# Loading a weight matrix in whole rows and copying it on chip, and holding one load of x back

## The chip, the core and the metric

The kernel runs on one core of a Trainium2 chip. The core has five engines that run their own instruction streams: TensorE (PE, matrix products; PEld is its weight load), VectorE (DVE), ScalarE (ACT), GpSimd (POOL) and SyncE (SP). Here SP and POOL also issue the transfers, which a set of 16 DMA engines carries out. SBUF is the on-chip memory with 128 partitions, PSUM the accumulators that TensorE writes.

The metric is the device time of one execution in microseconds, the median over several runs. The kernel before takes 698.39 us (three runs, 698.24 to 699.26).

## The reference

A short causal convolution, whose seven taps are a softmax over the kernel positions of each of 8 heads, feeds a two-layer network with a leaky ReLU between. Sizes: x is 8 x 4096 x 192 in float32, w_in is 192 x 2048, w_out is 2048 x 192.

```python
w = softmax(weight)                                   # 8 heads x 7 taps
x_pad = concatenate([zeros(B, 6, D), x])              # along the sequence
out = einsum('hk,bskhg->bshg', w, x_unf)              # head h owns 24 of the 192 channels
h = out.reshape(B * S, D) @ w_in
g = maximum(0.01 * h, h)
result = (g @ w_out).astype(float32)
```

## The kernel before

**Tiles.** Channels lie on partitions. The 192 channels make three chunks of 64 (`NCH = 3`, `CH = 64`), and two rows of the batch are processed together: row e=0 on partitions 0 to 63, row e=1 on partitions 64 to 127. A block is 512 positions of such a pair; there are 32. The first five blocks (`NHALF`) are worked in halves of 256 positions. Below, "half 0" to "half 3" are the first four: they are the first entries of `groups`, and the number is also the argument q of `load_first`. The outer loop runs over the groups with index i.

**Why w_in is needed twice in SBUF.** In `mm1` (L361) each row is a product of 64 partitions by 128 columns. For row e, both operands are read from partitions e\*64 to e\*64+63: `w_in[ps, c, ...]` and `y[ps, c, ...]`. So w_in stands in SBUF as [128, 3, 2048] in bf16, the same contents in both halves of the partitions. The copy in memory is float32; POOL's DMA converts it on the way.

**How w_in is loaded.** L234 to L241: four quarters of 512 columns, and for each one load for e=0 and one for e=1, all three chunks in one load. That makes eight DMAs on POOL's queue, each 64 partitions x 3 pieces of 2 KB. w_out follows on the same queue (L243).

**The start.** SP's queue takes the small `weight`, then x of halves 0 and 1 (`load_first`, L107, two DMAs each). A stage pool of two buffers holds these x tiles (`x_nat`). x of half 2 is issued at L335, after an explicit dependence on ScalarE's instruction `low` (L326). x of half 3 is issued at L340 and, as the pool has two buffers, waits until half 1's buffer has been read. `cast_first` turns each into bf16, `transpose_first` turns it on TensorE, and `evac_first` copies it into `xt`.

**The steady order.** For group i, the inner loop has T/64 steps. In each step TensorE runs `mm1` for two values of u, and ScalarE follows with one Prelu per u (L378), which turns the PSUM tile `ph` into `g`. Two `ph` buffers exist. Then come the slots of `mm2` (L391, product with w_out, operating on groups before), and VectorE gets a share of the convolution (L176, L182) of group i+1. In a half, one u covers 256 of the 2048 columns, so all 8 values of u need all of w_in. For half 0 the second matrix product has nothing to do yet; it starts in the first step of i=1. Inside i=0, after u=3, TensorE also does one chunk of the convolution of half 1 (`pe_ahead`). After the last step of i=0 come the cast of half 2's x on VectorE, its transposes and its copies to `xt`. In i=1 ScalarE casts half 3's x after u=0 and after u=2 (L462).

SP's queue is in program order: after the loads of the start it takes the output transfers and the transposing transfers of later blocks. POOL's queue goes on with `load_x` for block 2 and later (L79). It first waits, through a one-element copy (`pjunk`, L475), for the last g of half 0.

Of the kernel before, what the change touches and what calls it, by code (L numbers as in the profile page):

```python
# [14 lines left out]
def kernel(  # L15
# [8 lines left out]
    nc = tc.nc  # L24

    B, S, D = x.shape
    H, K = weight.shape
    Din, F = moe_w_in.shape
# [6 lines left out]
    CH = 64  # L35
    NCH = D // CH
# [5 lines left out]
    NB = S // ST  # L42
    NBLK = (B // 2) * NB
    LAG = NFC + NFC // 2
    WQ = 4
    NHALF = 5
    NPEC = 2

# [58 lines left out]
    def load_first(q, after=None):  # L107
        t = stage_pool.tile([128, 2, HS, D], FP32, name="x_nat")
        for e in range(2):
            ins = nc.sync.dma_start(  # L110
                out=t[:, e, :, :],
                in_=x[e, q * HT : (q + 1) * HT, :].rearrange("(c p) d -> p c d", p=128),
            )
            if after is not None and e == 0:
                tc.add_manual_dep(
                    ins.ins, after.ins.name,
                    mybir.DependencyInfo(
                        mybir.DependencyClass.Sync, mybir.DependencyReason.DATA
                    ),
                    reason="leave the DMA engines to w_in",  # L120
                )
        x_nat[q] = t

    def cast_first(q, e, copy):
        if q % 2 == 0 and e == 0:
            x_bf[q // 2] = xb_pool.tile([128, NCH, SUB, 2, CH], BF16, name="x_bf")
        h = q % 2
        copy(  # L128
            out=x_bf[q // 2][:, :, h * HS : (h + 1) * HS, e, :],
            in_=x_nat[q][:, e, :, :].rearrange("p s (c k) -> p c s k", c=NCH),  # L130
        )
# [20 lines left out]
    def evac_first(q, *copies):  # L152
        dst = xt[0][:, :, HALO + q * HT : HALO + (q + 1) * HT].rearrange(
            "p c (s i k) -> p i s c k", s=HS, i=2
        )
        for i, t in enumerate(ptr.pop(q)):
            copies[i](out=dst[:, i], in_=t)  # L157
# [4 lines left out]
    def conv_jobs(grp, chunks=range(NCH)):  # L162
        blk, t0, T = grp
        rp, st = divmod(blk, NB)
        if blk not in yt:
            yt[blk] = yt_pool.tile([128, NCH, ST], BF16, name="yt")
        y = yt[blk]
        jobs = []
        for c in chunks:
            for k in range(K):  # L170
                a = BASE + k + st * ST + t0
                src = xt[rp][:, c, a : a + T]
                dst = y[:, c, t0 : t0 + T]
                if k == 0:
                    jobs.append(
                        lambda s=src, d=dst, c=c: nc.vector.tensor_scalar_mul(  # L176
                            d, s, wk[:, c, 0:1]
                        )
                    )
                else:  # L180
                    jobs.append(
                        lambda s=src, d=dst, c=c, k=k: nc.vector.scalar_tensor_tensor(  # L182
                            out=d, in0=s, scalar=wk[:, c, k : k + 1], in1=d,
                            op0=mybir.AluOpType.mult, op1=mybir.AluOpType.add,
                        )
                    )
        return jobs
# [39 lines left out]
    for sign, off in ((1, 0), (-1, GRP - 1)):  # L227
        nc.gpsimd.affine_select(  # L228
            out=sel, in_=sel, compare_op=mybir.AluOpType.is_ge, fill=0.0,
            base=off, channel_multiplier=-sign * GRP,  # L230
            pattern=[[sign * CH, NCH], [0, 2], [sign, CH]],
        )

    w_in = const_pool.tile([128, NCH, F], BF16)  # L234
    for q in range(WQ):
        for e in range(2):
            fs = slice(q * F // WQ, (q + 1) * F // WQ)
            nc.gpsimd.dma_start(  # L238
                out=w_in[e * CH : (e + 1) * CH, :, fs],
                in_=moe_w_in[:, fs].rearrange("(c p) f -> p c f", p=CH),  # L240
            )  # L241
    w_out = const_pool.tile([128, NFC, D], BF16)
    nc.gpsimd.dma_start(out=w_out, in_=moe_w_out.rearrange("(c p) d -> p c d", p=128))  # L243

# [3 lines left out]
    def warm(n):  # L248
# [9 lines left out]
        out=nmax, in_=w9[:, 0:K], axis=mybir.AxisListType.X,  # L258
# [3 lines left out]
        out=w9[:, 0:K], in_=w9[:, 0:K], func=mybir.ActivationFunctionType.Exp,  # L262
# [33 lines left out]
    def diag_high(c):  # L296
        nc.vector.tensor_mul(
            diag[c][:, 0],
            ident2[:, None, :].to_broadcast([128, K, CH]),
            whm[:, c, 0, 0:K, None].to_broadcast([128, K, CH]),  # L300
        )

    def diag_low(c, ks):
        for k in ks:
            act = nc.scalar.activation(  # L305
                out=diag[c][:, 1, k, :], in_=ident2,
                func=mybir.ActivationFunctionType.Copy, scale=whm[:, c, 1, k : k + 1],
            )
        return act

    diag_high(0)
    cast_first(0, 0, nc.vector.tensor_copy)
    diag_low(0, range(2))
    cast_first(0, 1, nc.scalar.copy)
    transpose_first(0)
# [7 lines left out]
    wk = const_pool.tile([128, NCH, K], FP32, name="wk")  # L323
    nc.vector.tensor_mul(wk, wraw[:, :, 0:K], rsum.to_broadcast([128, NCH, K]))
    evac_first(0, nc.vector.tensor_copy, nc.scalar.copy)
    low = diag_low(0, range(2, K))  # L326
    diag_high(1)
    diag_low(1, range(K))

    def act_scale(out, in_, scale):  # L330
# [1 line left out]
            out=out, in_=in_, func=mybir.ActivationFunctionType.Copy, scale=scale  # L332
        )

    load_first(2, low)  # L335
    for n, job in enumerate(conv_jobs(groups[0], range(NPEC, NCH))):
        if n in (4, 5):
            cast_first(1, n - 4, nc.vector.tensor_copy)
        job()
    load_first(3)  # L340
    for c in range(NPEC):
        pe_jobs, evac_y = pe_conv_jobs(groups[0], c)
        for job in pe_jobs:
# [17 lines left out]
    def mm1(grp, u):  # L361
        blk, t0, T = grp
        y = yt[blk]
        nf = ST // T
        ph = psum_h.tile([128, 2, ST], FP32, name="ph", tag="ph")
        for i in range(nf):
            f = nf * u + i
            for c in range(NCH):
                for e in range(2):
                    ps = slice(e * CH, (e + 1) * CH)  # L370
                    nc.tensor.matmul(  # L371
                        out=ph[:, e, i * T : (i + 1) * T],
                        lhsT=w_in[ps, c, f * 128 : (f + 1) * 128],
                        rhs=y[ps, c, t0 : t0 + T],
                        start=(c == 0),
                        stop=(c == NCH - 1),
                    )
        act = nc.scalar.activation(  # L378
            out=g[blk][:, nf * u : nf * (u + 1), :, t0 : t0 + T],
            in_=ph.rearrange("p e (i t) -> p i e t", i=nf),  # L380
            func=mybir.ActivationFunctionType.Prelu, alpha=0.01,
        )
        while unsealed:
            seal[unsealed.pop()] = act.ins.name

    def mm2_one(rt, m, fc):
        b, e, s = subs[m]
# [52 lines left out]
    for i, grp in enumerate(groups):  # L440
        blk, t0, T = grp
        steps = T // 64
        if t0 == 0:
            g[blk] = g_pool.tile([128, NFC, 2, ST], BF16, name="g", tag="g")
        quota = (avail - slot) // steps

        if i == 0:
            ahead = []
        else:
            ahead = conv_jobs(groups[i + 1]) if i + 1 < len(groups) else []  # L450
        per = -(-len(ahead) // (steps - 1)) if T == ST else -(-len(ahead) // steps)
        for j in range(steps):
            for u in range(2 * j, 2 * j + 2):
                mm1(grp, u)
                if i == 0 and u == 0:
                    pe_ahead, evac_y = pe_conv_jobs(groups[1], 0)
                    ahead = conv_jobs(groups[1], range(1, NCH))
                    per = len(ahead)
                if i == 0 and u == 3:
                    for job in pe_ahead:  # L460
                        job()
                if i == 1 and u in (0, 2):  # L462
                    cast_first(3, u // 2, nc.scalar.copy)
            for _ in range(quota):
                mm2_slot(slot)
                slot += 1
            if i == 0 and j == 3:
                evac_y(nc.vector.tensor_scalar_mul)
                for e in range(2):
                    cast_first(2, e, nc.vector.tensor_copy)  # L470
                transpose_first(2)
                evac_first(2, nc.vector.tensor_copy, nc.vector.tensor_copy)
            if i == 1 and j == 1:

                nc.gpsimd.tensor_copy(out=pjunk, in_=g[0][0:1, NFC - 1, 1, HT - 1 : HT])  # L475
                load_x(2)
            if i == 2 and j == 1:
                transpose_x(2)
            for job in ahead[per * j : per * (j + 1)]:
                job()  # L480
            if i == 1 and j == 1:
                transpose_first(3)
                evac_first(3, nc.vector.tensor_copy, nc.vector.tensor_copy)

            last_half = t0 + T == ST
            if j == steps // 4 and last_half:
                load_x(blk + 3)
            if j == steps // 2 and last_half and blk > 0:
                transpose_x(blk + 2)
        avail += 2 * T // 128 * NFC  # L490
# [37 lines left out]
```

## Time and profile before

| What | Value |
|---|---|
| Median of the runs | 698.39 us |
| The profiled execution, its own time | 699.96 us |
| The profiled execution, first to last instruction (span) | 698.3 us |
| Mean granted TensorE clock | 0.997 |
| w_in loads, issue on POOL, eight | 626 ns each at the median, from 2.9 us to 8.0 us |
| w_in loads, issue to landing | 6.6 / 8.7 / 11.6 us (least, median, most) |
| w_out load, issue to landing | 14.7 us, from 9.77 us |
| x loads of the start (`x_nat`), issue to landing | 2.5 / 5.6 / 9.3 us |
| TensorE's wait for w_out | 1.8 us, once |
| TensorE's waits for w_in | 2.2 us at the weight load, 0.4 us at the matmul |
| HBM read | 29.88 MB |

The page gives each engine's busy time, then 40 equal slices of the span with tenths of busy time. In those slices the first tenth of the span has the highest DMA share (9, 9, 6, 9, 5), and TensorE is at 9 in all slices but the first and the last. Matmul spans overlap, so 9 means only that it always had work. The chain of work that ended last is followed back from the last instruction. "Issue to landing" is from the start of the issuing instruction to the moment when the last part of that transfer was reported as complete. The answers by stage give sums of busy time inside a stretch, in microseconds from the start of the span. The granted clock there is a share of TensorE's full clock.

### The profile page before, as it was taken

Reading aid. Unit: us, or ns where it says so; the run is one execution under the profiler, and the core shown is the slowest. Engines: PE = TensorE matmul, PEld = TensorE weight load, DVE = VectorE, ACT = ScalarE, POOL = GpSimd, SP = SyncE. Lnnn points to the kernel's source line nnn. Section 1 sums busy time; section 2 is a strip of 40 time slices with the busy share of each in tenths; the row PEclk is TensorE's granted clock in tenths of the full one; section 3 lists DMA queues with packets and bytes.
Section 4 is the critical chain, followed back from the end, with each engine's and each line's share of the span. In section 5 each row is a group of like instructions: output and inputs, shape, how many; then the busy total and the mean of one; then the engine's idle time right before and its main releaser. Section 6 shows DMA issues by size and latency. Waiting matters only on the chain.

```text
span 698.3 us, 26019 instructions
## 1 busy us (share of the span) xinstructions
PE 689.0 (99%) x11762; PEld 608.0 (87%) x11762; DVE 542.1 (78%) x1005; ACT 512.1 (73%) x576; POOL 142.3 (20%) x199
## 2 busy tenths in 40 slices
PE   8899999999999999999999999999999999999997
PEld 6799999678888888888888888888888888888887
DVE  7799999967777787777787777787777787777712
ACT  6688888977777777777777777777777777777770
POOL 4722220410222210222211222220222211000000
PEclk9999999999999999999999999999999999999999
DMA  9969554845555535555645556544566625122112
GB/s 170 115 83 104 83 71 81 86 71 76 77 74 83 89 67 76 77 74 84 86 67 79 69 81 81 88 73 71 77 75 81 92 63 77 54 52 58 47 36 69
DMA packets 184847, 54.39 MB, mean 78 GB/s; under 512 B 148384, under 2 KB 184736, under 8 KB 184736
## 3 DMA queue, kind: packets, MB, share of 16 engines
q0 software_dynamic: 98768, 14.17, 29.5%
q1 hardware_dynamic: 85968, 38.56, 23.2%
q8 instruction: 92, 1.51, 0.9%
q14 instruction: 19, 0.16, 0.1%
HBM read 29.88 MB, written 25.17 MB: 79 GB/s over the span
## 4 chain that ended last, share of the span: by engine, by line
PE 94%; DMA 3%; DVE 2%; POOL 0%; issue 0%; ACT 0%; POOLq 0%; ACTq 0%
PE po L391 48%; PE ph L371 46%; DMA w_out<-in_moe_w_out_dram 2%; DVE yt L182 2%; DMA w_in<-in_moe_w_in_dram 1%; POOL sel L228 0%; DVE yt L176 0%; ACT g L378 0%; POOL sel L226 0%; DVE o_sb L430 0%; POOL ident masks.py:199 0%; POOL ident masks.py:197 0%; PE ptr L143 0%; POOLq masks.py:199 0%; ACTq L430 0%
## 5 line engine op out<-in xcount | busy, mean ns | idle before, releaser
L378 ACT ACTIVATE g<-ph 128x1024 bf16<-128x1024 f32 x512 | 496.4, 1021 | 165.7 <-PE ph L371 165.7
L182 DVE SCALAR_TENSOR_TENSOR yt<-xt,wk,yt 128x512 bf16<-128x512 bf16 (+1 forms) x648 | 442.4, 683 | 17.6
L391 PE MATMUL po<-w_out,g 64*128 64x192 bf16 (+1 forms) x8048 | 398.4, 243 | 1.8 <-DMA w_out<-in_moe_w_out_dram 1.8
L391 PEld LDWEIGHTS <-g 64*128 64x128 bf16 (+1 forms) x8048 | 372.3, 94 | 31.1 <-issue 2.2
L371 PE MATMUL ph<-yt,w_in 64*128 64x512 bf16 (+1 forms) x3552 | 393.6, 348 | 2.2 <-ACT g L378 1.2
L371 PEld LDWEIGHTS <-w_in 64*128 64x128 bf16 x3552 | 247.8, 94 | 50.4 <-issue 3.9
L79 POOL DMA_DIRECT2D x_bf<-in_x_dram x180 | 133.7, 774 | 422.4 <-DMA xt<-x_bf 422.4
L430 DVE COPY o_sb<-po 128x192 f32<-128x192 f32 x216 | 77.2, 357 | 127.4 <-PE po L391 125.0
L176 DVE TENSOR_SCALAR yt<-xt,wk 128x512 bf16<-128x512 bf16 (+1 forms) x108 | 36.3, 336 | 0.1
L430 ACT COPY o_sb<-po 128x192 f32<-128x192 f32 x40 | 13.1, 327 | 0.0
L250 PE MATMUL warm<-zero 128*128 128x256 bf16 x24 | 5.2, 371 | 1.1 <-DVE junk L218 1.1
L157 DVE COPY xt<-ptr 128x384 bf16<-128x384 bf16 x7 | 2.2, 351 | 4.4 <-PE ptr L143 4.4
L201 PE MATMUL acc<-xt,diag 64*64 64x256 bf16 x84 | 5.2, 270 | 0.1
L238 POOL DMA_DIRECT2D w_in<-in_moe_w_in_dram x8 | 5.1, 643 | 0.0
L201 PEld LDWEIGHTS <-diag 64*64 64x64 bf16 x84 | 4.3, 106 | 0.8 <-DVE xt L157 0.4
L305 ACT ACTIVATE diag<-ident,whm 128x64 bf16<-128x64 bf16 x14 | 3.6, 335 | 1.9 <-DVE whm L291 1.9
L250 PEld LDWEIGHTS <-zero 128*128 128x128 bf16 x24 | 2.6, 125 | 2.1 <-DVE junk L218 1.1
L475 POOL COPY pjunk<-g 1x1 bf16<-1x1 bf16 x1 | 0.3, 312 | 10.9 <-ACT g L378 10.9
L143 PEld LDWEIGHTS <-x_bf 64*128 64x128 bf16 x48 | 1.4, 94 | 1.0 <-ACT x_bf L128 0.8
L143 PE MATMUL ptr<-ident,x_bf 64*128 64x64 bf16 x48 | 1.7, 191 | 0.5 <-DVE wraw L318 0.5
L128 DVE CAST x_bf<-x_nat 128x384 bf16<-128x384 f32 x5 | 2.2, 449 | 0.0
L255 ACT ACT_TABLE_LOAD x1 | 1.3, 1283 | 0.8 <-PEq L512 0.8
(34 smaller groups left out, 12.2 us busy)
## 6 DMA issues: line engine op xcount, KB each, us to landing
out_dram<-o_sb SPq DMA_DIRECT2D x128, 192.0 KB, 2.2
x_bf<-in_x_dram POOLq DMA_DIRECT2D x180, 64.0 KB, 3.1
x_nat<-in_x_dram SPq DMA_DIRECT2D x8, 192.0 KB, 5.6
w_in<-in_moe_w_in_dram POOLq DMA_DIRECT2D x8, 192.0 KB, 8.7
xt<-x_bf SPq DMA_TRANSPOSE x90, 2.4
w_out<-in_moe_w_out_dram POOLq DMA_DIRECT2D x1, 768.0 KB, 14.7
w<-in_weight_dram SPq DMA_DIRECT2D x1, 0.2 KB
```

Source lines behind the costliest of these rows:

```text
L79: nc.gpsimd.dma_start(out=t[:, c, :, e, :], in_=src[2 * rp + e, :, :, c * CH : (c + 1) * CH],)
L143: nc.tensor.transpose(out=ts[i][:, s, c, :], in_=x_bf[q // 2][ps, c, (q % 2) * HS + s, :, :].rearrange("p e k -> p (e k)"), identity=ident ...
L176: lambda s=src, d=dst, c=c: nc.vector.tensor_scalar_mul(d, s, wk[:, c, 0:1])
L182: lambda s=src, d=dst, c=c, k=k: nc.vector.scalar_tensor_tensor(out=d, in0=s, scalar=wk[:, c, k : k + 1], in1=d, op0=mybir.AluOpType.mult, ...
L201: lambda k=k, p=p, a=a, e=e, ps=ps: nc.tensor.matmul(out=acc[ps, :T], lhsT=diag[c][ps, p, k, :], rhs=xt[0][ps, c, a : a + T], start=(k == ...
L238: nc.gpsimd.dma_start(out=w_in[e * CH : (e + 1) * CH, :, fs], in_=moe_w_in[:, fs].rearrange("(c p) f -> p c f", p=CH),)
L250: nc.tensor.matmul(out=wa[:, 0, 0:HT], lhsT=zero[:, 0:128], rhs=zero, start=True, stop=True)
L305: act = nc.scalar.activation(out=diag[c][:, 1, k, :], in_=ident2, func=mybir.ActivationFunctionType.Copy, scale=whm[:, c, 1, k : k + 1],)
L371: nc.tensor.matmul(out=ph[:, e, i * T : (i + 1) * T], lhsT=w_in[ps, c, f * 128 : (f + 1) * 128], rhs=y[ps, c, t0 : t0 + T], start=(c == 0) ...
L378: act = nc.scalar.activation(out=g[blk][:, nf * u : nf * (u + 1), :, t0 : t0 + T], in_=ph.rearrange("p e (i t) -> p i e t", i=nf), func=my ...
L391: ins = nc.tensor.matmul(out=po[m], lhsT=g[b][ps, fc, e, s * 128 : (s + 1) * 128], rhs=w_out[ps, fc, :], start=(rt != 1 and fc == 0), stop ...
L430: copy(out=o_sb[:, n % 2, :], in_=po.pop(n))
```

## The change

Three things are changed.

w_in is fetched in three DMAs on POOL's queue, one for each chunk of 64 channels. Each writes partitions 0 to 63 with whole rows of 2048 columns. Three further DMAs on SP's queue copy each chunk from partitions 0 to 63 to partitions 64 to 127. They read what the first three wrote, so SP waits for the landing of each before it issues the copy.

x of half 2 no longer depends on `low`. It stands in SP's queue behind the three copies.

x of half 3 is issued later in the program: inside the main loop at i=0, u=2. It depends on the Prelu of that u, which `mm1` now returns.

```diff
-    WQ = 4
@@ load_first
-                    reason="leave the DMA engines to w_in",
+                    reason="leave the DMA engines to the weights",
@@
     w_in = const_pool.tile([128, NCH, F], BF16)
-    for q in range(WQ):
-        for e in range(2):
-            fs = slice(q * F // WQ, (q + 1) * F // WQ)
-            nc.gpsimd.dma_start(
-                out=w_in[e * CH : (e + 1) * CH, :, fs],
-                in_=moe_w_in[:, fs].rearrange("(c p) f -> p c f", p=CH),
-            )
+    for c in range(NCH):
+        nc.gpsimd.dma_start(out=w_in[0:CH, c, :], in_=moe_w_in[c * CH : (c + 1) * CH, :])
+    for c in range(NCH):
+        nc.sync.dma_start(out=w_in[CH:128, c, :], in_=w_in[0:CH, c, :])
     w_out = const_pool.tile([128, NFC, D], BF16)
     nc.gpsimd.dma_start(out=w_out, in_=moe_w_out.rearrange("(c p) d -> p c d", p=128))
@@ diag_low
-            act = nc.scalar.activation(
+            nc.scalar.activation(
...
-        return act
@@
-    low = diag_low(0, range(2, K))
+    diag_low(0, range(2, K))
@@
-    load_first(2, low)
+    load_first(2)
...
-    load_first(3)
@@ mm1
+        return act
@@ main loop
-                mm1(grp, u)
+                act = mm1(grp, u)
...
+                if i == 0 and u == 2:
+                    load_first(3, act)
```

## The prediction

> **What bounds the kernel now.** The page first: its busy table and its chain that ended last.
>
> ```profile
> span 698.3 us, 26019 instructions
> PE 689.0 (99%) x11762; PEld 608.0 (87%) x11762; DVE 542.1 (78%) x1005; ACT 512.1 (73%) x576; POOL 142.3 (20%) x199
> PE 94%; DMA 3%; DVE 2%; POOL 0%; issue 0%; ACT 0%; POOLq 0%; ACTq 0%
> ```
>
> TensorE sets the time; the only foreign link of any size is 3% DMA. The chain of the first 40 us places it:
>
> ```profile
> 2.90 6.58 DMA w_in<-in_moe_w_in_dram
> 9.48 0.28 issue
> 9.77 14.70 DMA w_out<-in_moe_w_out_dram
> 24.47 0.04 issue
> 24.51 1.33 PE po L391 x14
> ```
>
> POOL issued all eight w_in loads by 8.0, but w_out only at 9.77, after the first w_in load landed (9.48). w_out needed 14.7 us more, and TensorE, done with ph of the second half's first step at 22.4 us, stood until 24.47. Then the table by stage (PE, PEld, DVE, ACT, POOL busy, clock, DMA share, GB/s):
>
> ```profile
> 22.30:25.60 3.30, 1.50 (x23) 1.30 (x19) 3.12 (x7) 1.88 (x3) 3.30 (x5) 1.00 0.93 67
> 25.70:29.00 3.30, 3.30 (x32) 2.45 (x28) 1.46 (x3) 1.51 (x3) 3.30 (x6) 0.50 1.38 87
> 29.10:35.50 6.40, 6.40 (x146) 6.40 (x146) 4.76 (x11) 4.60 (x6) 6.39 (x9) 1.00 1.43 92
> 35.50:46.00 10.50, 10.50 (x230) 9.79 (x226) 9.82 (x24) 8.58 (x13) 0.00 (x0) 1.00 0.50 79
> ```
>
> The stand costs twice: after a stretch with 1.5 of 3.3 us busy the clock is at 0.50 for 3.4 us. From 29 us TensorE is full. So the change can only shift the point from which it is full, and everything behind it moves along. Last, VectorE's timeline for the third half (i=2), which becomes ready at the very end of this stretch:
>
> ```profile
> 20.70 0.62 DVE L157 COPY xt<-ptr 128x384 bf16<-128x384 bf16 x2 [1.14 <-PE ptr L143]
> 30.49 0.62 DVE L157 COPY xt<-ptr 128x384 bf16<-128x384 bf16 x2 [3.23 <-PE ptr L143]
> 32.61 3.09 DVE L182 SCALAR_TENSOR_TENSOR yt<-xt,wk,yt 128x256 bf16<-128x256 bf16 x6
> ```
>
> Its last convolution ends at 35.70; TensorE begins that half at 35.53 and waits 0.2 us for yt in the list of waits. VectorE also stood 3.2 us before 30.49, behind TensorE's stand. I use **35.7 us, third half ready** as the mark to compare.
>
> [...]
>
> **The change, part by part.**
>
> *POOL.* Eight issues of 0.64 us become three. Taken at the old 0.63 us each they end at 2.90+1.9=4.8, and w_out, ninth before and held by the first landing, is fourth: it is issued near 4.8 instead of 9.77.
>
> *Bytes.* w_in was fetched twice in float32, 8 x 0.39 = 3.15 MB; now 1.57 MB, plus 3 x 0.26 MB of bf16 copied on chip.
>
> *When the low half of w_in is in.* The DMA view, in stretches that hold one issue each, gives issue to landing of 6.6, 6.8, 7.1 and 8.4 us for the first four w_in loads, issued at 2.90, 3.65, 4.27 and 4.89: landings at 9.5, 10.4, 11.4 and 13.3. Four loads are 1.57 MB, just what the new kernel fetches. The fourth ran beside half 2's x, whose packets start at 11.5; at the spacing of the first three (0.95) it is 12.3. That is the upper value. The lower comes from two one-microsecond views:
>
> ```profile
> q0 software_dynamic: 103, 0.10, 84.1%
> q0 software_dynamic: 205, 0.19, 121.1%
> ```
>
> These are 6 to 7 us and 9 to 10 us. While the first two loads ran, both 2 KB slices of the same columns, half the bytes moved (0.10 against 0.19 MB of bf16). If whole rows remove this, 4 us at half rate become 2.3, so 10.6. I take 11.3 for the last chunk, some 10.1 and 9.0 for the others. Against it: half 1's x shares the queue with larger pieces; it landed at 8.3, and up to 1.5 us more is hidden, as yt then ends at 12.7 instead of 11.2, before any weights are whole.
>
> *The copies.* SP waits for each chunk in order, then issues. A 192 KB x load took 2.5 us alone, its first packet 1.0 us after issue. Half 2's came 3.5 us after issue, behind w_in packets of 1.211 x 16 / 205 = 95 ns. The copies stand behind w_out packets:
>
> ```profile
> q0 software_dynamic: 498, 0.19, 158.6%
> ```
>
> This is 20 to 21 us: 51 ns each, so about half of those 2.5 us, 1.3. [...]so 2.5+1.3 = 3.8, with 0.1 for SP's wait. Bounds: 2.5 (nothing ahead) to 5.5 (the three queue, 2 x 1.3 less the spacing of the chunks). w_in is whole at T = 11.3+3.9 = **15.2 us**. Until then TensorE has only two matmuls per piece, from about 11.3.
>
> *From T to the mark.* In the kernel before, ph's first matmul that had everything ran at 11.27, the first ACTIVATE of g at 12.03, and the third half's x was in place (evac at 20.70, ends 21.32) 9.3 us after that. In these 9.3 ScalarE waited 0.24 and 0.64 us for ph that w_in held up; these go. So T+0.7+8.4 = T+9.1. TensorE idles some 4 us before T, more than the 3.3 us that cost it half the clock before, so I add that: at half clock 12 matmuls of one u take 1.3 us, not 0.66, against ScalarE's 0.97 per u; 2.6 u in 3.4 us lose 0.9. Then VectorE: three chunks of seven convolution instructions, 3.33 each (21.35 to 24.68 in its timeline), are 10.0, and the copies of half 3 0.6. The mark is T+9.1+0.9+10.6 = T+20.6 = 35.8. TensorE itself arrives a little earlier: it is done with ph of the second half's first step at T+0.7+9.5+0.9 = T+11.1 (22.4 less 12.03 less the same 0.9), and four steps at full clock (ScalarE: two of 0.97 and 0.5 cast in the first two; then 2.63 each) take 9.2, T+20.3. VectorE ends last.
>
> *w_out.* Its 2048 packets (16 rows of 128 partitions) take 4.1 us at the 498 per us of 20 to 21 us; some 2 to 3.9 of copies and 1.5 of half 2's x (512 packets at some 47 ns over 16 engines) go in between: it is in at 19 to 22 us. It is wanted at T+11.1 = 26.3. Its stand of 2 us and the 1.7 us lost at half clock behind it go; what is late next is w_in itself.
>
> *Half 2's and half 3's x.* Half 2's needs no wait of its own but stands on SP behind the three copies: issued near 12.5 instead of 8.0, and with the old 7.7 to 9.3 in at 20 to 22, cast by VectorE near T+6 = 21. Half 3's waits for the third ACTIVATE of g, about T+3.7 = 19; nothing stands behind it on SP before the first output (35.96). Its cast sits on ScalarE at about T+10.4 = 25.6; with 2.5 to 5.6 us it is there. Cost nothing; with the 9.1 of the old busiest time, 2.4. POOL's loads of block 2 start 4 us later than 22.1; they took to about 29 and are transposed at 41.7, so the room is 12 us.
>
> **Sum.** 35.8 against 35.7: +0.1, and +0.2 for a copy that waits for the one before it: +0.3. The span goes from 698.3 to 698.6. The profiled run took 700.0, 1.7 more than its span, and the median of the runs is 698.39; the forecast is a shift of that: **698.7 us**.
>
> **Rivals.** *A, faster.* Whole rows stream at the full rate (10.6) and a copy takes 2.5: T=13.2, the idle time is 2 us and the clock stays: mark 13.2+9.1+10.6 = 32.9, -2.8, 695.6; at T=14 it is -2.0, 696.4. For: w_out's stand of 2.0 and the half clock after it are in the trace, and the total of bytes falls. Against: two DMAs in a row now stand before the first matmul, where one did.
>
> *B, slower: the copies hold the first ph.* Low rate throughout[...] or copies that share with w_out as half 2's x did with w_in (7.7 us): w_in low at 11.3 to 13, T=18. Mark 38.6, **+2.9, 701.3**. Place: TensorE's first ph. It is slower by over 0.2% from T=16.5. For: landings of 7.7 to 9.3 us under load. Against: w_out's packets are half as long.
>
> *C, half 3's x late* on ScalarE's queue, with every g behind it: +2.4, as above, 700.8. Against: 6 us of room.
>
> *D, no effect as meant:* w_out was hidden anyway. Excluded by 24.47.
>
> **How the numbers follow.** A measurement of this kernel tells 0.2% (1.4 us) from no change. Forecast, T between 13.7 and 16.5 at half clock for one stretch: 0.41. A: 0.24. B: 0.30, C: 0.05. Faster 0.24, same 0.41, slower 0.35. The likeliest alone spans 697.0 to 699.8; the range for 8 in 10 takes in most of A and B up to T=18.8: 695.8 to 702.2.
>
> **What would show it.** Right: w_out lands before TensorE wants it; the first ACTIVATE of g is at 15 to 17 us and none of the first eight waits for w_in; half clock near 15 to 19 instead of 25.7 to 29; the mark within 1.4 us of 35.7. Wrong: w_in copies landing after 16.5 or before 13.7, w_out still ahead of TensorE's second step, a wait for x_nat on ScalarE, or any gap of TensorE after 40 us that is new.

## The result, and the profile after

The changed kernel takes 706.17 us (median of four runs, 705.94 to 706.4); the kernel before, beside it, 698.83 (698.24 to 700.08). The ratio is 1.0103, with a 95% interval of 1.0085 to 1.012. The prediction was 698.7, with 695.8 to 702.2 as its range: the change costs 7.3 us where +0.3 was forecast.

The page of the kernel after (span, busy times, and the chain that ended last, first by engine and then by line):

```profile
span 704.6 us, 26019 instructions
PE 688.8 (98%) x11762; PEld 609.5 (86%) x11762; DVE 542.1 (77%) x1005; ACT 512.3 (73%) x576; POOL 138.7 (20%) x194
PE 83%; DVE 13%; DMA 2%; issue 1%; POOL 0%; ACT 0%; POOLq 0%; ACTq 0%
PE po L387 42%; PE ph L366 41%; DVE yt L181 12%; DMA w_in<-w_in 1%; DMA w_in<-in_moe_w_in_dram 1%; DVE yt L175 1%; ACT g L373 0%; PE acc L200 0%; DVE xt L156 0%; POOL w_in L236 0%; POOL sel L227 0%; POOL sel L225 0%; DVE o_sb L426 0%; POOL ident masks.py:199 0%; PE ptr L142 0%
```

TensorE does the same work in a longer span. w_out, a link of the chain before, is gone from it. In order of time, the chain of the kernel after has two DMAs in a row ahead of TensorE's first product:

```profile
4.09 7.74 DMA w_in<-in_moe_w_in_dram
11.84 8.64 DMA w_in<-w_in
20.52 4.53 PE ph L366 x34
```

The last chunk of w_in landed at 11.8 us. Its copy was issued at once and landed 8.64 us later, at T = 20.48. The list of waits names who stood (us in total, times, longest):

```profile
ACT g L373 <- PE ph L366: 171.3, 251, 10.1
PEld L366 <- DMA w_in<-w_in: 9.1, 3, 6.7
PE ph L366 <- DMA w_in<-w_in: 8.3, 3, 6.5
```

TensorE stood three times, once for each copy. ScalarE stood 10.1 us before its first Prelu. The page's table of DMA issues (KB each, us to landing) of the kernel after:

```profile
w_in<-in_moe_w_in_dram POOLq DMA_DIRECT2D x3, 256.0 KB, 7.0
w_out<-in_moe_w_out_dram POOLq DMA_DIRECT2D x1, 768.0 KB, 16.7
w_in<-w_in SPq DMA_DIRECT2D x3, 256.0 KB, 8.7
```

In this kernel, with w_out beside it, a 256 KB copy between two halves of SBUF takes longer than a 256 KB load from memory that is also converted (that KB is of the bf16 side). The table by stage, in the columns of the prediction, shows TensorE's clock in and after its stand:

```profile
11.00:14.60 3.60, 0.40 (x15) 0.20 (x13) 3.36 (x9) 0.47 (x1) 0.00 (x0) 0.96 1.36 189
14.60:20.00 5.40, 0.79 (x4) 0.21 (x4) 3.96 (x9) 0.00 (x0) 0.00 (x0) 0.50 1.16 199
20.00:25.00 5.00, 4.48 (x45) 2.98 (x45) 0.00 (x0) 2.88 (x3) 0.00 (x0) 0.54 0.07 19
25.00:31.00 6.00, 5.43 (x100) 4.61 (x100) 1.61 (x5) 4.60 (x6) 0.00 (x0) 1.00 0.23 68
```

The clock is at half from about 14.3 to 24.6 us. The first part falls on idle time, but after 20.5 TensorE, with work at last, does it at half speed. VectorE's timeline of the kernel after ends the account:

```profile
26.75 0.48 DVE L206 TENSOR_SCALAR yt<-acc,rsum 128x256 bf16<-128x256 f32 x1 [7.94 <-PE acc L200]
30.53 0.62 DVE L156 COPY xt<-ptr 128x384 bf16<-128x384 bf16 x2 [2.63 <-PE ptr L142]
38.55 3.09 DVE L181 SCALAR_TENSOR_TENSOR yt<-xt,wk,yt 128x256 bf16<-128x256 bf16 x6
```

VectorE now stands behind TensorE for 7.9 us, and the third half is ready at 38.55 + 3.09 = 41.64 us instead of 35.70. This mark moves everything behind it. From the mark to the end of the span it is 663.0 us; in the profile of before it was 662.6, and in all the profiles of the experiments it is 662.9 to 663.8.

### The profile page after: what moved, and what is told of

Read it like the earlier page. It is cut to its first block, busy times and chain, and to the rows that moved or that the text cites. A ratio compares the mean times of both kernels' runs of the same rounds, so it can differ in the third digit from the quotient of the medians.

```text
span 704.6 us, 26019 instructions
## 1 busy us (share of the span) xinstructions
PE 688.8 (98%) x11762; PEld 609.5 (86%) x11762; DVE 542.1 (77%) x1005; ACT 512.3 (73%) x576; POOL 138.7 (20%) x194
## 4 chain that ended last, share of the span: by engine, by line
PE 83%; DVE 13%; DMA 2%; issue 1%; POOL 0%; ACT 0%; POOLq 0%; ACTq 0%
PE po L387 42%; PE ph L366 41%; DVE yt L181 12%; DMA w_in<-w_in 1%; DMA w_in<-in_moe_w_in_dram 1%; DVE yt L175 1%; ACT g L373 0%; PE acc L200 0%; DVE xt L156 0%; POOL w_in L236 0%; POOL sel L227 0%; POOL sel L225 0%; DVE o_sb L426 0%; POOL ident masks.py:199 0%; PE ptr L142 0%
```

## The experiments

"Mark" below is the end of the third half's last convolution, "T" the moment when all of w_in stands in both halves of the partitions. Ratios are against the kernel before on the same chip.

**1. w_out out of the way.** In the changed kernel, w_out is issued only after the first Prelu:

```diff
-    nc.gpsimd.dma_start(out=w_out, in_=moe_w_out.rearrange("(c p) d -> p c d", p=128))
@@ main loop, after mm1 for i == 0 and u == 0
+                    ld = nc.gpsimd.dma_start(
+                        out=w_out, in_=moe_w_out.rearrange("(c p) d -> p c d", p=128)
+                    )
+                    tc.add_manual_dep(ld.ins, act.ins.name, ...)
```

> The changed kernel, but w_out is issued only after the first Prelu of half 0, so that nothing of POOL's queue is ahead of the three copies. Queueing theory (the copies took 8.7 us because w_out's packets stood before and between them): each copy lands 2.5 to 3.5 us after its issue, the last one near 14.5 to 15 us instead of 20.5, and the time falls to 699 to 701 us. Slow-copy theory (192 pieces of 4 KB between the two halves of the partitions need 5.5 us by themselves): the last copy lands at 17 us or later and the time stays above 702 us. In both, w_out lands some 7 us after the first Prelu, before or close to the 25 us at which it is wanted.

Measured: 701.67 us (701.3 to 702.29), ratio 1.0053 [1.0038, 1.0068]. Its chain of waits:

```profile
4.08 8.12 DMA w_in<-in_moe_w_in_dram
12.22 4.05 DMA w_in<-w_in
16.31 4.25 PE ph L365 x43
```

The last copy took 4.05 us instead of 8.64, though w_in itself landed no earlier (12.2 against 11.8). T is 16.26, the mark 37.14; TensorE does not wait for w_out. T and the time lie between the two expectations: queueing alone would have given 14.5 to 15 us, slow copies alone 17 us or more. One microsecond of this kernel's DMA view while the copies run without w_out (packets, MB, and the time of the packets as a share of the 16 engines' time):

```profile
DMA packets 65, 0.20 MB, mean 205 GB/s; under 512 B 15, under 2 KB 15, under 8 KB 65
q1 hardware_dynamic: 65, 0.20, 91.8%
```

At 205 GB/s the 0.26 MB of one copy are an estimate of 1.3 us. So the copies have two prices: their own rate, and w_out. The copies' packets in the two traces split the difference of 4.2 us in T:

| Copies | w_out after them | w_out ahead, as in the change |
|---|---|---|
| first issued | 9.78 us | 8.92 us |
| first packet after that | 1.2 us | 4.7 us |
| first to last packet (192 of 4 KB) | 4.4 us | 5.9 us |
| reported complete after that | 0.9 us | 1.0 us |

Here 3.5 us are a late first packet, 1.5 us a longer stretch from the first packet to the last, and 0.9 us come back because the first chunk landed earlier. The packets themselves are hardly longer (296 ns at the mean against 281). They are spread out, with w_out's between them.

**2. The dose.** Half of w_out is issued early, the other half after the first Prelu:

```diff
-    nc.gpsimd.dma_start(out=w_out, in_=moe_w_out.rearrange("(c p) d -> p c d", p=128))
+    nc.gpsimd.dma_start(out=w_out[:, 0 : NFC // 2, :], in_=w_rows[:, 0 : NFC // 2, :])
@@ main loop, after mm1 for i == 0 and u == 0
+                    ld = nc.gpsimd.dma_start(
+                        out=w_out[:, NFC // 2 :, :], in_=w_rows[:, NFC // 2 :, :]
+                    )
```

> The changed kernel with the first half of w_out left where it is and the second half issued after the first Prelu of half 0 (the dose between the changed kernel and the one with all of w_out late). Queueing theory: the wait of the copies grows with w_out's packets that are in flight, so the last copy lands about halfway between 16.3 and 20.5 us, at 17.5 to 19, and the time is 703 to 705 us. If instead any w_out ahead costs the full delay (a fixed start-up loss), it lands at 20 us and the time is 706 us; if the first half is through before the copies start, it lands at 16.5 us and the time is near 701.7 us.

Measured: 705.38 us (704.22 to 705.98), ratio 1.0105 [1.009, 1.0121]. The copies took, from issue to landing:

```profile
DMA to landing us min/median/max: 6.9/7.2/7.6
```

T is 18.75, between 16.26 (none of w_out early) and 20.48 (all of it). The first packet comes 3.4 us after its issue. That w_out delays the copies is shown by the three doses. The total follows less clearly. The profiled execution took 704.22 us, the least of the four; the median is only 0.8 us under the change, above the 703 to 705 expected, and its ratio is that of the change.

**3. The same bytes in smaller loads.** w_out is still issued at once, in four DMAs:

```diff
-    nc.gpsimd.dma_start(out=w_out, in_=moe_w_out.rearrange("(c p) d -> p c d", p=128))
+    for k in range(4):
+        ks = slice(k * NFC // 4, (k + 1) * NFC // 4)
+        nc.gpsimd.dma_start(out=w_out[:, ks, :], in_=w_rows[:, ks, :])
```

> The changed kernel with w_out's one load split into four loads of 4 chunks each, still issued on POOL right behind w_in (near 4.6, 5.3, 6.0 and 6.7 us), so that all of w_out's bytes are queued before the first copy is issued near 8.9 us, as before. Theory [...]that the size of w_out's load decides how late the copies' first packets are: the first copy packet comes 1 to 2.5 us after its issue instead of 4.3, the copies land 1.5 to 3 us earlier, T near 18 to 19, third half ready near 39 to 40, 703.5 to 705. Rival, that the copies only share the engines with whatever bytes w_out has queued: the first packet still 4 us late, T 20 to 20.8, third half ready 41 to 42, 705.5 to 706.7.

Measured: 705.25 us (704.79 to 705.92), ratio 1.0098 [1.008, 1.0117]. The copies' row:

```profile
DMA to landing us min/median/max: 7.8/8.0/8.0
```

The first packet still comes 4.1 us after its issue; T is 19.21, the mark 40.23. T and the time lie between the two expectations, but the late first packet, on which they differed, did not go: how w_out is cut is at most a small part (0.7 us of the landing). It may be none: in the profile of experiment 7, where w_out is one load as in the change, the first packet came after 4.1 us too and the copies took 7.9 to 8.4. The runs show the delay, not what sets it.

**4. Whole rows alone.** The three copies are taken away; each chunk's rows are fetched twice:

```diff
     for c in range(NCH):
-        nc.gpsimd.dma_start(out=w_in[0:CH, c, :], in_=moe_w_in[c * CH : (c + 1) * CH, :])
-    for c in range(NCH):
-        nc.sync.dma_start(out=w_in[CH:128, c, :], in_=w_in[0:CH, c, :])
+        for e in range(2):
+            nc.gpsimd.dma_start(
+                out=w_in[e * CH : (e + 1) * CH, c, :], in_=moe_w_in[c * CH : (c + 1) * CH, :]
+            )
```

> The changed kernel without copies: each chunk of w_in is fetched from memory in whole rows twice, once for each half of the partitions, on POOL's queue ahead of w_out. If the copies are the whole loss, w_in is complete near 16 us (3.15 MB at the 0.95 us per 0.39 MB of the kernel before, from 9.5 us on), half 0 starts there, and the time is 700 to 702 us: slower than before, as the first product needs all of w_in and no longer only its first quarter, but faster than the changed kernel. If whole rows were at fault, w_in would be complete only after 19 us and the time would stay at 705 us.

Measured: 702.92 us (702.41 to 703.62), ratio 1.0071 [1.0056, 1.0086]. TensorE's timeline of this kernel:

```profile
14.19 0.28 PE L367 MATMUL ph<-yt,w_in 64*128 64x256 bf16 x1 [1.20 <-DMA w_in<-in_moe_w_in_dram]
15.61 0.28 PE L367 MATMUL ph<-yt,w_in 64*128 64x256 bf16 x1 [1.14 <-DMA w_in<-in_moe_w_in_dram]
17.01 2.31 PE L367 MATMUL ph<-yt,w_in 64*128 64x256 bf16 x19 [1.12 <-DMA w_in<-in_moe_w_in_dram]
```

One load after the other releases one matmul. A quarter of the columns lets a product be finished; a chunk of the channels only lets it begin, as every product sums over all three chunks. So T is 16.97 here, and the first Prelu runs at 18.08. In the profile of the kernel before that experiment 6 gives, the last load lands later (18.19), yet the first Prelu ran at 12.36. The total is 4.9 us above the kernel before (702.92 less 698.0), without any copy, and 0.9 us above the range expected. Not all of it is the order by chunks: the moved loads of x are in this kernel too, and TensorE's clock was at half from 16.5 to 19.9 us.

**5. The same fetch with copies that no queue holds up.** VectorE copies the chunks instead of the DMA:

```diff
-    for c in range(NCH):
-        nc.sync.dma_start(out=w_in[CH:128, c, :], in_=w_in[0:CH, c, :])
@@ around evac_first(1, ...)
+    for c in range(2):
+        nc.vector.tensor_copy(out=w_in[CH:128, c, :], in_=w_in[0:CH, c, :])
     evac_first(1, nc.vector.tensor_copy, nc.vector.tensor_copy)
+    nc.vector.tensor_copy(out=w_in[CH:128, 2, :], in_=w_in[0:CH, 2, :])
```

> The changed kernel with the copies on VectorE in place of DMAs; w_out stays early. Queueing theory: VectorE has the chunks over by 13 to 15 us (three copies of 64 x 2048 bf16, [...]the last one after the landing at 11.8), nothing waits for w_out (in by 19 us), and the time is 696 to 698.5 us, faster than before. Slow-copy theory: the same, as it concerns DMAs alone. A third theory, that any early w_out slows the start in itself by holding back x of half 2, expects more than 702 us.

Measured: 700.06 us (698.96 to 701.79, twelve runs), ratio 1.0028 [1.0015, 1.0041]. VectorE's timeline:

```profile
11.54 1.29 DVE L343 COPY w_in<-w_in 64x2048 bf16<-64x2048 bf16 x2
...
13.51 0.69 DVE L345 COPY w_in<-w_in 64x2048 bf16<-64x2048 bf16 x1
```

0.65 to 0.69 us for a copy that took the DMA 3.4 to 4.3 without w_out and 8.7 in the change. T is 14.2, the mark 35.25. Against the kernel before beside each, the loss falls from 7.3 us to 2.1. It does not become the gain that was expected (696 to 698.5 us): the first Prelu runs at 14.9, 2.5 us later than with quarters (12.36, experiment 6). A part is the clock (0.63 of full from 14 to 18 us). The four of the twelve runs with a mean clock of 0.999 or more took 698.96 to 699.46, still above the kernel before.

**6. The kernel before, profiled once more.**

> The kernel before, profiled once more. Of 23 runs of it 21 had a mean clock of 0.999 or 1.0 and spans of 695.6 to 697.5 us, two had 0.997 and 699.3 and 699.5; the profile that the prediction was made from had 0.997 and 698.3. If that profile was of the rarer kind, this one shows no half clock between 25 and 29 us, a span near 696.3, and the third half ready at 33.5 to 34.5 us instead of 35.7. If the half clock is the rule and the difference lies elsewhere, it shows 35.7 again.

One execution took 698.59 us, span 696.9. Its table by stage, and its VectorE timeline:

```profile
22.40:24.00 1.60, 0.00 (x0) 0.00 (x0) 1.49 (x4) 1.46 (x3) 1.60 (x3) 1.00 0.72 49
24.00:27.40 3.40, 3.38 (x52) 3.21 (x53) 2.81 (x7) 1.21 (x2) 3.40 (x6) 1.00 1.26 80
27.40:35.50 8.10, 8.10 (x185) 8.10 (x182) 6.77 (x16) 6.68 (x10) 7.75 (x11) 1.00 1.43 103
```

```profile
28.33 0.62 DVE L157 COPY xt<-ptr 128x384 bf16<-128x384 bf16 x2 [1.34 <-PE ptr L143]
...
30.10 3.09 DVE L182 SCALAR_TENSOR_TENSOR yt<-xt,wk,yt 128x256 bf16<-128x256 bf16 x6
```

TensorE stands for w_out as it did (1.6 us), but the clock stays at 1.00 afterwards, and the mark is 33.19, not 35.70. Of 91 runs of the kernel before that were timed beside the experiments, 79 have a mean clock of 0.999 or more, with a median of 698.07 us; 12 have 0.995 to 0.998, with a median of 700.3. The execution that the prediction was built on took 699.96 at 0.997: it was one of the rarer kind. Against the median of all 91, 698.13, the change costs 8.0 us. Both cases are profiled here: a stand of 1.8 us with half clock behind it for 3.4 us, and one of 1.6 us with none. What decides between them is not shown, nor that it was this stand in the other runs with a lower clock.

**7. Keeping the clock in the stand.** 60 matmuls on zeros go before the first product of the changed kernel:

```diff
     evac_first(1, nc.vector.tensor_copy, nc.vector.tensor_copy)
+    warm(60)
```

> The changed kernel with 60 idle matmuls (on zeros, results unused) on TensorE just before half 0's first product, which fill some 6.5 us of the 9 us in which it stands. Clock theory (a part of the loss is that the long stand drops the clock to half for two stretches, 15.8 to 22.6 us in the changed kernel): the mean clock rises from 0.992-0.995 to 0.997 or more, the first eight ACTIVATEs of g come at 0.97 us each from the start, and the time falls by 1 to 2.5 us, to 703.5 to 705 us. Theory that only the late landing of the copies counts: the copies land at 20.5 as before and the time stays within 0.7 us of 706.2.

Measured: 706.28 us (704.5 to 708.1), ratio 1.0105 [1.0081, 1.0128]. Two of the four runs kept the clock at 0.999 to 1.0 and took 704.5 and 705.1; two had 0.997 and took 707.46 and 708.1. In the profiled one, with the clock kept, the mark is T + 20.1 (20.17 and 40.26), against T + 21.2 in the change, whose half clock lasts from 14.3 to 24.6 us. So the clock's share is near 1.1 us in that trace; as a whole this run settles nothing, since the times of the other two are not explained.

**8. Half 3's x held back, alone.** In the kernel before:

```diff
-    load_first(3)
@@ main loop, after mm1
+                if i == 0 and u == 2:
+                    load_first(3, act)
```

> The kernel before with one part of the change alone: x of half 3 is issued after the third Prelu of half 0. Both theories: 0.39 MB fewer stand between w_in and w_out, so the last w_in load lands about 1 us earlier and w_out some 1 us earlier (23.4 instead of 24.5); 697 to 698.5 us. If holding x back were what costs, ScalarE would wait for it before its first cast in half 1 and the time would be 701 us or more.

Measured: 699.57 us (697.56 to 702.01, twelve runs), ratio 1.0017 [1.0003, 1.0031]. The last w_in load landed at 18.82 us and w_out at 24.14 (18.19 and 23.97 in experiment 6), so neither came earlier as expected, and TensorE still stood 1.6 us for w_out. Six of the twelve runs have a mean clock of 0.997 or less, more than usual for the kernel before; the other six take 697.56 to 699.46, like it. The x load alone neither helps w_out nor costs anything that these runs can show apart from the clock.

**9. Other places for the copies.** These keep the quarters, fetch each once into partitions 0 to 63, and copy on an engine. GpSimd first; here half 3's x is also held back:

```diff
+    for q in range(WQ):
+        fs = slice(q * F // WQ, (q + 1) * F // WQ)
+        nc.gpsimd.tensor_copy(out=w_in[CH:128, :, fs], in_=w_in[0:CH, :, fs])
```

> A version against both kernels: w_in in four column quarters as in the kernel before, but fetched once, into partitions 0 to 63, and each quarter copied to partitions 64 to 127 by GpSimd (which does nothing from 6 to 21 us); w_out follows the four loads at once; x of half 3 held back. Theory that the whole-row order is the other half of the loss (no product before all of w_in is there): the first quarter is in at 9.5 us and copied by 11 to 11.5, half 0 starts within 0.5 us of the kernel before, w_out lands by 19 us and TensorE does not wait for it: 694.5 to 696.5 us. If GpSimd's copies of 64 x 1536 bf16 take over 2.5 us each, u=2 and later wait for them and the time is 697 us or more.

Measured: 701.83 us (700.8 to 703.15), ratio 1.0043 [1.0026, 1.0059]. GpSimd's timeline, then VectorE's, of this kernel:

```profile
8.18 1.46 POOL L245 COPY w_in<-w_in 64x1536 bf16<-64x1536 bf16 x1 [1.46 <-DMA w_in<-in_moe_w_in_dram]
11.08 4.54 POOL L245 COPY w_in<-w_in 64x1536 bf16<-64x1536 bf16 x3 [1.44 <-DMA w_in<-in_moe_w_in_dram]
```

```profile
8.15 2.81 DVE L182 SCALAR_TENSOR_TENSOR yt<-xt,wk,yt 128x256 bf16<-128x256 bf16 x3
10.88 0.42 DVE L128 CAST x_bf<-x_nat 128x384 bf16<-128x384 f32 x1
11.21 1.61 DVE L182 SCALAR_TENSOR_TENSOR yt<-xt,wk,yt 128x256 bf16<-128x256 bf16 x1
12.75 1.68 DVE L128 CAST x_bf<-x_nat 128x384 bf16<-128x384 f32 x1
```

Beside a GpSimd copy, a convolution instruction of 0.48 us takes 1.61 and a cast of 0.42 takes 1.68. Why is not shown. The copies were free for GpSimd and not for VectorE, which the convolution needs. The mark of this kernel is 38.28.

Next, all four on VectorE; the first goes after the first half's convolution, the others after `evac_first(1, ...)`:

```diff
+    copy_w(0, nc.vector.tensor_copy)
...
     evac_first(1, nc.vector.tensor_copy, nc.vector.tensor_copy)
+    for q in range(1, WQ):
+        copy_w(q, nc.vector.tensor_copy)
```

> A version against both kernels: the quarters of the kernel before, fetched once into partitions 0 to 63, and copied to partitions 64 to 127 on VectorE (GpSimd's copies had slowed VectorE); x of halves 2 and 3 as in the kernel before. Four copies of 64 x 1536 bf16 at about 0.5 us (0.65 us for 2048 columns was measured). w_out lands near 18 us, TensorE does not stand for it, and no run has the half clock. VectorE's chain to the third half becomes the bound: 2 us more work there against the 0.7 and 1.3 us that it stood in the kernel before, third half ready at 32.5 to 33.2 us instead of 33.2: 697.3 to 698.5 us. If VectorE had hidden room, 695.5 to 697 us; if the first copy holds up half 0's first product by more than 1 us, 699 us.

Measured: 699.96 us (699.63 to 700.83, ten runs), ratio 1.0029 [1.002, 1.0038]. Nothing waits for w_out, the clock is at least 0.999 in every run, and the mark is 35.14: from 12.7 us on, VectorE's own chain is the bound.

The last quarter is then copied on ScalarE, after u=3 of half 0:

```diff
                 if i == 0 and u == 3:
+                    copy_w(WQ - 1, nc.scalar.copy)
```

> The same, with the last quarter's copy on ScalarE after the fourth Prelu of half 0, where it stood 1.4 us in the kernel before while TensorE did a chunk of the convolution. [...]ScalarE hides it, VectorE's chain is 0.5 us shorter: 696.8 to 698 us, 0.3 to 0.5 us below the version with all four on VectorE. If the copy takes longer than the gap, the fifth Prelu comes later and the time is above that version's.

Measured: 699.22 us (698.85 to 699.82, 21 runs), ratio 1.0013 [1.0005, 1.0021]; mark 34.81.

At last quarter 0 is fetched for both halves as before, and only quarters 1 to 3 are copied:

```diff
+        for e in range(2 if q == 0 else 1):
...
+    for q in range(1, WQ - 1):
+        copy_w(q, nc.vector.tensor_copy)
```

> The kernel before with its quarters of w_in fetched once, into partitions 0 to 63, except quarter 0, which is fetched for both halves as before; quarters 1 and 2 are copied to partitions 64 to 127 on VectorE after the first map's eviction of half 1, quarter 3 on ScalarE after the fourth Prelu of half 0. Theory that the second fetch of w_in is worth little and VectorE's chain decides: the two copies add 1.25 us to VectorE where it stood 2.0 us in the kernel before, the third half is ready near 32.5 (33.2 in the kernel before without the half clock), w_out is in by 19 and TensorE doesn't wait for it: 697.2 to 698.2 us, from the same to 0.8 us faster than before. Rival: the 0.39 MB more ahead of the copies delays the first of them, or VectorE is still the bound of the conv's evictions: 698.5 to 699.2 us, as with all four quarters copied.

Measured: 699.14 us (697.6 to 700.87, 14 runs), ratio 1.0003 [0.9991, 1.0016]; mark 34.88 in its profile, later than the 32.5 expected. It is not faster than the kernel before. No version tried is.

The marks of these last three versions hold one more thing. In their profiles the first chunk of half 0's convolution on TensorE, 28 matmuls, took 2.9 to 3.2 us; in both profiles of the kernel before it took 1.7. The first line is from the kernel before, the second from the version with ScalarE:

```profile
7.00 1.73 PE L201 MATMUL acc<-xt,diag 64*64 64x256 bf16 x28
7.53 3.17 PE L201 MATMUL acc<-xt,diag 64*64 64x256 bf16 x28
```

In the second, most of them start 106 ns apart instead of 54, as at half clock, though the tables give the clock of this stretch as 1.00. The first Prelu comes at 13.7 to 14.1 us instead of 12.36, which is most of what these marks lose against 33.19. In the last version VectorE then needs 21.8 us from its copy of half 1's x to the mark, and 21.6 in experiment 6. The profiles of experiments 1, 3 and 4 began as slowly, but there the first product waits for w_in in any case. How often an execution begins so, the run times do not show. So these marks are no measure of the copies on VectorE and ScalarE, and why the last versions do not win stays open.

## Why the prediction was wrong

The sum of the prediction was T = 15.2, mark = T + 20.6, and a shift of the mark against 35.7. Point by point:

- *POOL's issues and w_in in the low half:* right. w_out was issued at 4.59 (4.8 predicted), the last chunk landed at 11.82 (11.3). Cost of the difference: 0.5 us. (In the working, 4 us at 0.10 against 0.19 MB become 2.1, not 2.3; nothing rests on it.)
- ***The copies:* this term failed.** It was put at 3.8 us and bounded by 5.5; it is 8.64. The 2.5 in its sum was the time of a 192 KB load of x; that a copy takes as long was the author's estimate, which no row of before shows. The size fits copies without w_out (3.4 to 4.3 us, experiment 1), but it was meant for copies with w_out ahead of them. "About half of those 2.5 us, 1.3" was allowed for w_out ahead of them. The price was worked out from one w_out packet's length (51 ns against 95). The number queued was left out of this price: in the trace some 1300 of w_out's 2048 packets moved before the first of the copies did, and w_out then went on between them. The upper bound let the three copies queue behind each other, but added no more of w_out than these 1.3. The right size was in the trace of before: half 2's x, issued behind w_in, took 7.7 to 9.3 us, and the prediction set this aside because "w_out's packets are half as long". With the copies and the landing of w_in as measured, T is 20.48 instead of 15.2.
- *From T to the mark:* right in size, 20.6 predicted, 21.2 measured; 20.1 to 21.2 across the kernels that load whole rows. The clock was at half for three stretches of 3.4 us and not for one, but most of that fell on idle time.
- *The baseline:* wrong. "Its stand of 2 us and the 1.7 us lost at half clock behind it go" counted both as a gain. The stand is in either profile of the kernel before (1.6 us in experiment 6), but its usual executions do not have the loss at half clock. The forecast was a shift of the median, but the shift was measured from a profile 1.6 us above it (699.96 against 698.39). With the mark of experiment 6, 33.2, the same sum gives 35.8 - 33.2 = 2.6 us slower, with the copies still priced at 3.8.

The sum of these: 5.3 for T (4.8 of it the copies), 0.6 for the clock and what follows T, 1.6 for the baseline, 7.5 in all; 706.17 less 698.7 is 7.5.

- *w_out, half 2's x, half 3's x:* right. w_out landed at 21.27 and was first used at 32.10; half 2's x landed at 21.6; half 3's x was issued at 25.22 and landed by 28.12, without a wait on ScalarE (rival C didn't happen).
- *Rival B* had the place (TensorE's first ph), the cause ("copies that share with w_out") and the sign, and it decided from T = 16.5. Only its price was short: T = 18, where the change gave 20.5.
- *Rival A* could not occur in this form: even without w_out, T is 16.26, where A needed 13.2 to 14. That the clock stays after 2 us of idling was its estimate; in the two profiles of the kernel before, one of two stands of 1.6 and 1.8 us was followed by half clock.

One more loss was seen and not weighed; "what is late next is w_in itself" was written down without a price. The old order made the first quarter complete at about 10 us, and TensorE began while six loads were on their way. Experiment 4 gives up to 4.9 us for this, before any copy.

What stays open: why the first packet of a copy waits for so much of w_out (the cut into four didn't remove it), the exact share of the clock in 706.17, and what moving half 2's x cost by itself, as it was not run alone (no instruction waits for that load in the profile of the change).

## What to carry to other kernels

A DMA that must wait for another's landing can find in front of it what was issued in the meantime, on another queue too, as these copies found w_out (the last landed 8.64 us after its issue, and 4.05 with w_out out of the way). So count the bytes queued there and allow for them, and put a bulky transfer that nobody wants yet behind it. Cut a weight so that each piece finishes a product; pieces of the summed dimension complete no product until the last is in (one matmul per load, and the first Prelu at 18.08 us instead of 12.36, in experiment 4). Before a forecast is made as a shift, set the profiled execution beside the median, and don't count as a gain a loss that only that execution had.

## What was not expected of the hardware

- A copy of 256 KB between partition halves by DMA: 4.0 us without w_out (205 GB/s while the copies ran), 8.7 us with 0.79 MB of w_out queued. Most of the delay is before the first packet (4.7 us instead of 1.2); the 4 KB packets themselves took 296 ns at the mean instead of 281. VectorE does the same copy in 0.65 to 0.69 us.
- A copy of 64 x 1536 in bf16 between the halves took 0.62 to 0.69 us on VectorE, 1.47 on ScalarE and 1.46 on GpSimd, and the last more than tripled the time of VectorE's instructions beside it.
- The stand of 1.6 to 1.8 us in the kernel before was followed by half clock in one of two profiles. Of 91 runs 12 have a mean clock below 0.999, and they take some 2 us more.
- TensorE can also begin at half its pace: in six of the profiles here the first 28 matmuls of the convolution, begun near 7.4 us, took 2.6 to 3.2 us instead of 1.7, and the mean clock of the run does not show it.
